# The sign of 64-bit weights placed by one ScalarE rectifier instead of a ScalarE copy and a VectorE max

## The chip, the core and the metric

The kernel runs on one core of one Trainium2 chip. The core has a matrix engine (TensorE, written PE in the profile, with its weight loads as PEld), three engines for elementwise work (VectorE: DVE; ScalarE: ACT; GpSimd: POOL) and a queue that issues the transfers (SyncE: SP). The metric is the time of one execution on the device, in microseconds (us). Lower is better.

## What is computed

Three blocks follow each other over a batch of 4 sequences of 576 tokens: windowed attention with 8 heads of 64, a gated block with a mixing matrix over the sequence, and a squared-rectifier block with a gate. Cut to what matters:

```python
# attention, per batch and head: a band of 128 keys with a linear bias
scores = where(mask, q @ k.T / 8 + bias, -1e9);  attn = softmax(scores);  x = attn @ v
# gated block
h = gelu(x @ w_in); u, v = split(h); v = layernorm(v) * g_ln
x = x + (u * (w_sg @ v + b_sg)) @ w_out
# last block
xk = mu_k * x + (1 - mu_k) * x_prev;  xr = mu_r * x + (1 - mu_r) * x_prev
out = sigmoid(xr @ w_r) * (relu(xk @ w_k) ** 2 @ w_v)
```

The five matrices `w_in`, `w_out`, `w_k`, `w_v` and `w_r` arrive as 64-bit floats. The kernel reads each weight as two 32-bit words, builds a 32-bit float out of them, and splits that into a high and a low part for the matrix engine. Building the 32-bit float is called the decode below.

## The kernel before, in words

The program first records all operations with the tiles that they read and write, then a list scheduler (the planner, `Rec.schedule`) decides at build time in which order each engine runs them and, for operations that may run on several engines, on which. An operation has a cost, a due time worked back from the matrix work that needs it, and a correction from the table `PRI` (lines 29 to 35), which is looked up by the name of the first tile that the operation writes and by its engines. Two entries are of use here: `("st0", "act"): -57000` and `("st1", "act"): 4000` (in ns; a negative one makes an operation more urgent). On the chip each engine runs its list in order and waits where an input or a buffer isn't ready.

Work in the order of time. Attention of batch 0 comes first, alone, with the loads and the decode of `w_in`. Then three rounds follow in which the gated block of batch b runs beside the attention of batch b+1; the decode of `w_out` falls into the first of these. The gated block of the last batch runs with the decode of `w_k`. Last comes the third block in five chunks of tokens (`phase2`), at whose start `w_r` and `w_v` are decoded.

One decode is one call of `job` (line 544) on 128 rows and 512 columns (256 for `w_out`); there are 8 of `w_in`, 8 of `w_out`, 8 of `w_k`, 4 of `w_r` and 8 of `w_v`, 36 in all. `lo` and `hi` are the two words of each weight, interleaved in the loaded tile `raw`. The steps of a job:

- line 548: SP loads `raw`. For `w_in` its place is in the standing tiles `st0` and `st1`; otherwise it is a buffer of a ring (`wraw`).
- line 553: ACT multiplies `hi`, read as a 32-bit float, by 2^-112, in place in `raw`.
- line 554: DVE writes the tile `w` (named `wdec`): the larger of `hf` and `hf * -2^32`, which puts the sign at a bit that survives the next step.
- line 555: DVE shifts `w` left by 3. Line 556: DVE merges the top bits of `lo`.
- line 564: a copy to the high part, on ACT, DVE or POOL; line 565: the rest to the low part, on DVE or POOL.

The tile `wdec` is one of 4 buffers while `w_in` is decoded (a ring that the gated block uses too, tag `t`), one of 2 for `w_out`, and a single buffer for `w_k`, `w_r` and `w_v` (`dec=("raw2", "wdec")`). A job can write it only when the job whose buffer it takes over has finished line 565. In the listing, line 553 doesn't touch `wdec`, so ACT can do it as soon as the load has landed.

Lines of helpers stand for many operations in the rows: L399 is any ACT function of `K.act`, L455 is `stt` (a DVE instruction with two inputs), L472 is `ts` on DVE, L419 is `tt` on DVE, L407 and L409 are copies on ACT and DVE, L427 is a square on ACT, and L377 is every matmul.

Of the kernel before, what the change touches and what calls it, by code (L numbers as in the profile page):

```python
# [13 lines left out]
ACTF = mybir.ActivationFunctionType  # L14
ALU = mybir.AluOpType
# [64 lines left out]
class Vw:  # L80
# [25 lines left out]
    def real(self):  # L106
        t = self.base
        if t.real is None:
            t.real = t.rec.open_pool(t.pool).tile(list(t.shape), t.dtype, tag=t.tag, name=t.name, bufs=t.bufs)
        a = t.real  # L110
        for k, x in self.ops:
            if k == "ix":
                a = a[x]
            elif k == "bc":
                a = a.bitcast(x)
            elif x == 3:
                a = a.rearrange("p a b -> p (a b)")
            elif x == 4:
                a = a.rearrange("p a b c -> p (a b c)")
        return a  # L120
# [374 lines left out]
def attn_gmlp_rwkv_kernel(  # L495
# [18 lines left out]
    nc = tc.nc  # L514
    K = Build(nc)
# [11 lines left out]
    def T(pool, shape, dtype, tag, name=None, bufs=None):  # L527
        return R.tile(pool, shape, dtype, tag, name or tag, bufs)
# [15 lines left out]
    def job(dst_h, dst_l, src, n, dup=False, raw=None, dec=("wraw", "wdec")):  # L544
        if src.dtype != F32:
            if raw is None:
                raw = T(stage[0][0], [P, n, 2], U32, stage[0][1], "wraw")
            K.dma(raw.flat()[:, 0:2 * n], src.bitcast(U32), P * n * 8)
            lo, hi = raw[:, :n, 0], raw[:, :n, 1]
            w = T(dec[0], [P, n], F32, dec[1], "wdec", bufs=4 if dec[0] == "tp" else (2 if dec[0] == "wraw" else 1))  # L550
            wu = w.bitcast(U32)
            hf = hi.bitcast(F32)
            K.act(hf, hf, ACTF.Copy, scale=2.0 ** -112)
            K.stt(w, hf, -(2.0 ** 32), hf, ALU.mult, ALU.max)
            K.ts(wu, wu, 3, None, ALU.logical_shift_left, None)
            K.stt(wu, lo, 29, wu, ALU.logical_shift_right, ALU.bitwise_or, cost=68 + n / 0.96)
        else:
            w = T(stage[0][0], [P, n], F32, stage[0][1], "wraw")
            if dup:
                K.dma(w[0:64], src, 64 * n * 4)  # L560
                K.dma(w[64:128], src, 64 * n * 4)
            else:
                K.dma(w, src, P * n * 4)
        K.copy(dst_h, w, "adp")
        K.sub(dst_l, w, dst_h)
# [8 lines left out]
    def sg_job(kk, half):  # L574
        c = slice(half * HS, half * HS + HS)
        src = w_sgT[kk * P:min(S, kk * P + P), c]
        job(w_sg_t[:, kk, 0, c], w_sg_t[:, kk, 1, c], src, HS, dup=kk == 4)

    def out_job(kk, half):
        c = slice(half * 256, half * 256 + 256)  # L580
        job(w_out_t[:, kk, 0, c], w_out_t[:, kk, 1, c], cols(w_out, kk, half), 256)
# [417 lines left out]
    def phase2(w_k_t):  # L999
# [42 lines left out]
        for kk in range(NC):  # L1042
            job(w_r_t[:, kk, 0, :], w_r_t[:, kk, 1, :], rows(w_r, kk), DM, dec=("raw2", "wdec"))
# [185 lines left out]
```

## Time and profile before

| | us |
|---|---|
| median of 3 runs | 627.09 |
| lowest and highest of them | 625.8, 627.79 |
| the profiled execution, its own time | 628.37 |
| span of the profiled execution | 626.6 |

The span is what the trace covers; 1.77 us of the profiled execution's time lie outside it. Its own time is 1.28 us above the median. Busy times are those of an engine's instructions, without its queue's work. The windows cut the span into stretches by time; the granted clock of TensorE (PEclk) is 1.00 at 2.4 GHz and 0.50 at 1.2 GHz. The chain of waits goes back from the last instruction to whatever released each step.

### The profile page before, as it was taken

How to read it: one execution, taken by the hardware profiler on the slowest of the kernel's cores; microseconds unless marked ns; L12 is line 12 of the kernel's file. 1: busy time of each engine (PE TensorE's matmuls, PEld its weight loads, DVE VectorE, ACT ScalarE, POOL GpSimd, SP SyncE). 2: the span in 40 equal slices, each digit the busy share in tenths (PEclk: the TensorE clock that was granted, in tenths of full speed). 3: DMA queues.
4: the chain of work that ended last, by engine and by line, in shares of the span. 5: the costliest groups of instructions: out<-in, count | busy, mean ns of one | idle time of the engine just before them, and what ended most of it. 6: DMA issues, size and time to landing. Idle time of an engine off the chain costs nothing.

```text
span 626.6 us, 10161 instructions
## 1 busy us (share of the span) xinstructions
PE 595.6 (95%) x3458; PEld 498.7 (80%) x3458; DVE 475.6 (76%) x1286; ACT 352.0 (56%) x912; POOL 189.4 (30%) x348
## 2 busy tenths in 40 slices
PE   8776988997999999999999999899999999999997
PEld 4454867895889998899989998688888887888896
DVE  5888799997999998999689999996384229326122
ACT  5988688785798567883337339744330332234031
POOL 5676375432664354642325430000000001000000
PEclk9987999996999999999999999999999999999999
DMA  8961421432513316010081238433002000000100
GB/s 308 311 218 52 141 69 49 154 94 84 170 56 98 97 40 211 21 61 12 1 274 42 97 112 266 129 109 102 33 2 84 18 0 35 33 1 1 52 18 33
DMA packets 25332, 57.74 MB, mean 92 GB/s; under 512 B 4416, under 2 KB 13120, under 8 KB 24768
## 3 DMA queue, kind: packets, MB, share of 16 engines
q1 hardware_dynamic: 25280, 57.09, 27.7%
q8 instruction: 27, 0.44, 0.3%
q14 instruction: 25, 0.20, 0.1%
HBM read 47.63 MB, written 9.45 MB: 91 GB/s over the span
## 4 chain that ended last, share of the span: by engine, by line
PE 76%; DVE 11%; ACT 7%; DMA 3%; issue 2%; POOL 1%; SPq 0%; POOLq 0%; ACTq 0%; DVEq 0%
PE d L377 41%; PE vps L377 16%; PE rps L377 7%; PE s L377 5%; PE a L377 5%; PE tf L385 2%; ACT p L399 2%; DMA rawqk<-in_qk_dram 2%; DVE p L680 2%; DVE wdec L455 1%; DMA wraw<-in_w_r_dram 1%; ACT pf L407 1%; DVE QK L419 1%; ACT p L482 1%; POOL pf L438 1%
## 5 line engine op out<-in xcount | busy, mean ns | idle before, releaser
L377 PE MATMUL d<-xk,wk 128*128 128x512 f32 (+1 forms) x480 | 105.1, 368 | 0.0
L377 PEld LDWEIGHTS d<-xk,wk 128*128 128x128 f32 x480 | 84.7, 188 | 16.0
L377 PE MATMUL vps<-w_v_t,k2h 128*128 128x512 f32 x288 | 93.9, 396 | 0.0
L399 ACT ACTIVATE p<-p,nmax 128x256 f32<-128x256 f32 (+3 forms) x160 | 76.6, 480 | 24.7 <-DVE nmax L680 23.5
L438 POOL TENSOR_SCALAR_AFFINE_SELECT pf<-pf 128x384 f32<-128x384 f32 (+2 forms) x85 | 51.3, 608 | 50.7 <-ACT pf L407 48.5
L680 DVE CUSTOM_DVE_ANT_0 p<-s,mask 128x256 f32<-128x256 f32 (+3 forms) x160 | 59.9, 380 | 8.4 <-PE s L377 8.2
L377 PE MATMUL d<-w_sg_t,vhl 128*128 128x288 f32 x448 | 65.9, 298 | 0.0
L399 ACT ACTIVATE rl<-d 128x512 f32<-128x512 f32 (+1 forms) x40 | 22.1, 554 | 76.3 <-PE d L377 73.4
L377 PEld LDWEIGHTS vps<-w_v_t,k2h 128*128 128x128 f32 x288 | 54.2, 188 | 12.9 <-DVE r L419 0.3
L377 PE MATMUL d<-w_in_t,xg 128*128 128x512 f32 (+1 forms) x240 | 60.9, 402 | 0.3 <-ACT x L407 0.3
L377 PEld LDWEIGHTS d<-w_sg_t,vhl 128*128 128x128 f32 x448 | 60.7, 188 | 0.6 <-issue 0.2
L377 PE MATMUL d<-gg,w_out_t 128*128 128x288 f32 x384 | 56.8, 299 | 3.6 <-DVE gg L419 3.6
L377 PE MATMUL d<-xg,w_in_t 128*128 128x288 f32 x384 | 56.2, 298 | 1.7 <-DVE u L455 1.3
L377 PE MATMUL rps<-w_r_t,xr 128*128 128x512 f32 x216 | 54.6, 392 | 2.8 <-ACT w_r_t L407 1.4
L377 PE MATMUL vps<-w_v_t,k2l 128*128 128x512 f32 x144 | 57.0, 396 | 0.0
L377 PEld LDWEIGHTS d<-gg,w_out_t 128*128 128x128 f32 x384 | 52.5, 190 | 4.7 <-DVE gg L419 3.9
L409 DVE CAST k2h<-rl 128x512 fp32r<-128x512 f32 (+1 forms) x29 | 11.3, 389 | 59.0 <-ACT rl L427 59.0
L377 PEld LDWEIGHTS d<-xg,w_in_t 128*128 128x128 f32 x384 | 52.1, 188 | 3.2 <-DVE u L455 1.8
L377 PEld LDWEIGHTS d<-w_in_t,xg 128*128 128x128 f32 (+1 forms) x240 | 41.8, 180 | 12.4 <-ACT x L407 0.6
L377 PEld LDWEIGHTS rps<-w_r_t,xr 128*128 128x128 f32 x216 | 40.1, 188 | 12.2 <-ACT w_r_t L407 1.9
L419 DVE TENSOR_TENSOR r<-vps,r 128x512 f32<-128x512 f32 x18 | 12.4, 690 | 46.9 <-PE vps L377 46.8
L421 POOL TENSOR_TENSOR p<-p 128x128 f32<-128x128 f32 (+1 forms) x62 | 33.5, 543 | 38.7 <-ACT p L399 32.3
(119 smaller groups left out, 1176.6 us busy)
## 6 DMA issues: line engine op xcount, KB each, us to landing
rawqk<-in_qk_dram SPq DMA_DIRECT2D x32, 576.0 KB, 4.1
rawv<-in_v_dram SPq DMA_DIRECT2D x32, 160.0 KB, 2.7
xs<-x SPq DMA_DIRECT2D x4, 1154.0 KB, 5.3
out_dram<-r SPq DMA_DIRECT2D x18, 256.0 KB, 2.0
st<-in_w_in_dram SPq DMA_DIRECT2D x8, 512.0 KB, 7.1
wraw<-in_w_k_dram SPq DMA_DIRECT2D x8, 512.0 KB, 3.8
wraw<-in_w_v_dram SPq DMA_DIRECT2D x8, 512.0 KB, 3.5
wraw<-in_w_out_dram SPq DMA_DIRECT2D x8, 256.0 KB, 2.6
```

What stands on the lines that cost most here:

```text
L377: pe.matmul(real(o), real(l), real(r), start=st, stop=sp, **ex)
L385: pe.transpose(real(o), real(i), real(d))
L399: nc.scalar.activation(real(out), real(in_), func, scale=scale, **kw)
L407: alts.append(("act", self._act(in_), lambda: nc.scalar.copy(real(out), real(in_))))
L409: alts.append(("dve", self._dve(in_.n, not in_.ps), lambda: nc.vector.tensor_copy(real(out), real(in_))))
L419: alts.append(("dve", self._dve(out.n, False), lambda: nc.vector.tensor_tensor(real(out), real(a), real(b), op)))
L421: alts.append(("pool", 140 + 2.12 * out.n, lambda: nc.gpsimd.tensor_tensor(real(out), real(a), real(b), op)))
L438: nc.gpsimd.affine_select(out=real(out), in_=real(in_), pattern=[[0, rows], [sgn, n]], compare_op=cmp, fill=0.0, base=0, channel_multiplie ...
L455: alts.append(("dve", cost or self._dve(out.n, False, isinstance(s, Vw)), lambda: nc.vector.scalar_tensor_tensor(real(out), real(a), real( ...
L482: alts.append(("act", self._act(a, 1), lambda: nc.scalar.mul(real(out), real(a), real(s1))))
L680: K.raw("dve", 70 + w / 0.96, lambda: nc.vector.tensor_tensor_reduce(out=real(pw), in0=real(si), in1=real(ma), scale=-0.125, scalar=3.0e38 ...
```

## The change

In `job`, the ACT instruction of line 553 and the DVE instruction of line 554 become one ACT instruction: the leaky rectifier `Prelu`, whose input is `hf` times 2^-112, whose slope for negative inputs is -2^32, and which writes `w`. `raw` isn't written any more after the load. In the record the operation now reads `hf` and writes `wdec`, where line 553 wrote `raw` (`st0`, `st1` or `wraw`). It is given to the planner with the same cost as line 553 had. Nothing else in the text of the kernel changes.

```diff
@@ -550,8 +550,8 @@
             w = T(dec[0], [P, n], F32, dec[1], "wdec", bufs=4 if dec[0] == "tp" else (2 if dec[0] == "wraw" else 1))
             wu = w.bitcast(U32)
             hf = hi.bitcast(F32)
-            K.act(hf, hf, ACTF.Copy, scale=2.0 ** -112)
-            K.stt(w, hf, -(2.0 ** 32), hf, ALU.mult, ALU.max)
+            K.raw("act", K._act(hf), lambda: nc.scalar.activation(
+                real(w), real(hf), ACTF.Prelu, scale=2.0 ** -112, alpha=-(2.0 ** 32)), [hf], [w])
             K.ts(wu, wu, 3, None, ALU.logical_shift_left, None)
             K.stt(wu, lo, 29, wu, ALU.logical_shift_right, ALU.bitwise_or, cost=68 + n / 0.96)
```

## Rows read from the trace of the kernel before

**Rows 1.** The page's busy times: engine, busy us, share of the span, instructions.
```profile
PE 595.6 (95%) x3458; PEld 498.7 (80%) x3458; DVE 475.6 (76%) x1286; ACT 352.0 (56%) x912; POOL 189.4 (30%) x348
```

**Rows 2.** Windows by stage: length, busy PE, PEld, DVE, ACT, POOL, PEclk, DMA.
```profile
0.00:64.00 64.00, 48.61 (x230) 29.70 (x231) 51.28 (x182) 49.72 (x155) 43.37 (x86) 0.87 0.66 219
64.00:100.00 36.00, 32.07 (x198) 25.71 (x198) 32.53 (x90) 28.41 (x77) 20.38 (x41) 0.99 0.28 89
100.00:145.00 45.00, 40.47 (x311) 36.80 (x309) 43.43 (x131) 36.10 (x106) 19.33 (x36) 0.98 0.33 104
145.00:312.00 167.00, 166.58 (x1202) 147.15 (x1204) 150.90 (x450) 115.47 (x340) 77.52 (x150) 0.97 0.25 80
312.00:380.00 68.00, 68.00 (x440) 62.66 (x437) 63.03 (x124) 32.76 (x64) 24.57 (x32) 1.00 0.40 132
380.00:402.00 22.00, 19.15 (x83) 14.92 (x82) 21.34 (x43) 18.90 (x35) 0.00 (x0) 1.00 0.65 208
402.00:627.00 225.00, 220.76 (x1005) 181.80 (x1003) 113.12 (x272) 70.68 (x139) 4.23 (x5) 1.00 0.12 40
```

**Rows 3.** Groups of DVE by shape: count, busy us, mean ns, idle before.
```profile
L455 DVE SCALAR_TENSOR_TENSOR wdec<-wraw 128x512 f32<-128x512 f32 x20 | 13.6, 682 | 0.7 <-ACT wraw L399 0.7
...
L455 DVE SCALAR_TENSOR_TENSOR wdec<-st 128x512 f32<-128x512 f32 x8 | 7.7, 962 | 0.4 <-ACT st L399 0.4
...
L455 DVE SCALAR_TENSOR_TENSOR wdec<-wraw 128x256 f32<-128x256 f32 x8 | 4.9, 609 | 0.0
```

**Rows 4.** Groups of ACT by shape, the same columns.
```profile
L427 ACT ACTIVATE rl<-rl 128x512 f32<-128x512 f32 x32 | 19.9, 632 | 0.8
...
L399 ACT ACTIVATE wraw<-wraw 128x512 f32<-128x512 f32 x20 | 13.6, 682 | 9.2 <-DMA wraw<-in_w_k_dram 6.8 <-DMA wraw<-in_w_v_dram 1.8 <-DMA wraw<-in_w_r_dram 0.7
...
L399 ACT ACTIVATE st<-st 128x512 f32<-128x512 f32 x8 | 5.4, 670 | 0.0
...
L399 ACT ACTIVATE wraw<-wraw 128x256 f32<-128x256 f32 x8 | 3.5, 439 | 0.4 <-DMA wraw<-in_w_out_dram 0.4
...
L399 ACT ACT_TABLE_LOAD x2 | 2.6, 1283 | 0.8 <-PEq L1216 0.8
```

**Rows 5.** Chain of waits, 0 to 64 us, by line.
```profile
by line: ACT p L399 13.1%; PE s L377 13.0%; PE a L377 12.4%; DMA rawqk<-in_qk_dram 7.1%; ACT pf L407 5.6%; issue 5.3%; DVE p L680 5.3%; PE tf L385 5.0%; ACT p L482 4.9%; ACT st L399 4.7%; POOL pf L438 4.0%; DVE p L419 3.2%; ACT x L407 2.0%;
```

**Rows 6.** Chain of waits, 110 to 162 us: by line, then start, us, what.
```profile
by line: PE d L377 12.6%; DVE wdec L455 11.7%; DMA rawqk<-in_qk_dram 9.9%; PE s L377 9.2%; PE a L377 6.1%; DVE w_out_t L419 5.9%; issue 5.7%; DVE p L680 5.5%; ACT QK L407 4.2%; DVE vsg L455 3.9%; PE tf L385 3.3%; DVE gg L419 2.7%; DVE KL L4
...
130.70 1.55 DVE wdec L455
...
136.07 0.67 DVE KL L419
...
136.77 5.17 DMA rawqk<-in_qk_dram
...
142.02 1.15 ACT QK L407
```

**Rows 7.** Timeline of PE: start, us, instruction, idle before it.
```profile
145.06 1.33 PE L377 MATMUL d<-gg,w_out_t 128*128 128x288 f32 x4 [3.62 <-DVE gg L419]
...
396.86 0.73 PE L377 MATMUL rps<-w_r_t,xr 128*128 128x512 f32 x2 [1.44 <-ACT w_r_t L407]
...
400.88 5.74 PE L377 MATMUL rps<-w_r_t,xr 128*128 128x512 f32 x24 [1.23 <-ACT r L399]
```

**Rows 8.** Windows of PE, 2 us each: busy, PEclk, DMA share, GB/s.
```profile
142.00:144.00 2.00, 0.00 (x0) 0.88 0.00 0
144.00:146.00 2.00, 0.94 (x4) 0.50 0.02 4
...
150.00:152.00 2.00, 2.00 (x10) 0.50 0.02 9
...
154.00:156.00 2.00, 2.00 (x21) 1.00 0.38 154
```

**Rows 9.** Timelines of ACT and DVE near 384 us.
```profile
384.39 0.69 ACT L399 ACTIVATE wraw<-wraw 128x512 f32<-128x512 f32 x1
...
384.65 0.68 DVE L419 TENSOR_TENSOR w_r_t<-wdec,w_r_t 128x512 fp32r<-128x512 f32 x1
```

## The prediction, made before the changed kernel was seen

> **What bounds the kernel now.** I read the busy times first [rows 1]. PE is busy for 595.6 of 626.6 us, so all that elementwise work can cost or give back is the remaining 31 us, plus what PE loses at the lower clock. DVE comes second with 475.6 us, but a share of the whole says little here, because the stages have different limits. So I cut the span at the borders of its stages [rows 2]; in each row the reader should subtract PE's busy time from the length, and then see which other engine is full.
>
> - 0 to 64 us: PE idles for 15.4 us. DVE has 51.3 and ACT 49.7 of 64 us; neither is full.
> - 64 to 100: PE idles for 3.9 us, DVE has 32.5 of 36.
> - 100 to 145: PE idles for 4.5 us and DVE is full (43.4 of 45).
> - 145 to 380: PE idles for 0.4 us in 235. Whatever happens on another engine here is hidden, unless it makes PE wait.
> - 380 to 402: PE idles for 2.9 us and DVE is full (21.3 of 22).
> - 402 to the end at 626.6: PE idles for 3.8 us, DVE has half of its time free.
>
> So time is to be had in the first 145 us and around 390 us. Next I read the chain of waits in these stretches. From 0 to 64 us [rows 5] ACT carries more of it than DVE: softmax on ACT (`p` L399 and L482, 18.0% together), copies of `pf` and `x` (7.6%) and the scaling of line 553 (`st` L399, 4.7% of 64 us, or 3.0 us), against 8.5% for the two largest of DVE. From 110 to 162 us [rows 6] it is a DVE chain: the decode's two-input instructions (`wdec` L455) alone are 11.7% of 52 us, which is 6.1 us. At its end stand the low half of the keys (KL) at 136.07 us, a load of `rawqk` that is issued at 136.77, after KL has let go of a buffer, and takes 5.17 us, and the copy to QK at 142.02. Meanwhile PE runs dry: 3.62 us of idle time before 145.06 [rows 7], and behind it the granted clock is 0.50, the lower of its two levels, from 144 to 152 us [rows 8], which costs about half of 8 us, 4.0 us. The two shorter gaps of 1.44 and 1.23 us near 400 us [rows 7] lie in a stage with a granted clock of 1.00 [rows 2].
>
> **What is removed.** The 36 DVE instructions of line 554: 20 of 0.682 us, 8 of 0.962 and 8 of 0.609 [rows 3], 13.6 + 7.7 + 4.9 = 26.2 us of DVE. By stage: the 8 of `w_in` (7.7 us) fall into 0 to 64, the 8 of `w_out` (4.9) into 100 to 145, the 8 of `w_k` (5.5) into 312 to 380, 5 of the third block (3.4) into 380 to 402 and the last 7 (4.8) behind it. The 10.3 us behind 402 and in 312 to 380 are worth nothing in themselves: PE is full there [rows 2]. If that cover went, the 5.5 us of `w_k` would count at most once.
>
> **What is added.** The ACT instructions stay at 36: 20 of 0.682, 8 of 0.670 and 8 of 0.439 us [rows 4]. The function changes and the output is now contiguous, where it had a step of two words. The trace doesn't show the rectifier. Bounds: the square of a contiguous tile of the same size takes 0.632 us and the strided copy 0.682 [rows 4]. I take 0.67, as the input keeps its stride, so ACT's load is the same within 36 x 0.05 = 1.8 us either way, which I leave at 0 in the sum. No load, queue entry of SP or matmul is added or removed.
>
> **What is moved, and the new wait.** The sign step now runs on ACT and writes `wdec`. Line 553 only had to wait for its load: at 384.39 us ACT does it while DVE has yet to finish the job before, at 384.65 [rows 9]. The rectifier must wait until the buffer of `wdec` is free. With 4 buffers (`w_in`) or 2 (`w_out`) that is far off. With the single buffer of the last 20 jobs, each rectifier waits for line 565 of the job before, and behind it in ACT's list stand the rectifiers of the matmul results `d` and, through these, PE. This is the cost that the trace doesn't show. Below: nothing, if the planner gives ACT other work meanwhile. Above: for each of the 4 jobs of `w_r`, one further ACT instruction in front, 0.632 us [rows 4], 2.5 us together on the chain that sets when PE may begin `rps`. Against it, DVE is rid of 3.4 us in the same 22 us, and it is DVE that is full there.
>
> **The plan is made anew.** Durations at build time change, so every list behind the first `w_in` job may come out in another order. Also, the operation is now called `wdec` and misses the two entries of `PRI` for `st0` and `st1`. The four scalings with -57000 were pulled ahead of softmax work; without it they yield to what is due sooner. Since 3.0 us of them lie on the ACT chain [rows 5], I expect no harm from this, but the rows can't exclude it.
>
> **The sum**, against the profiled execution's own time, 628.37 us (the span 626.6 and 1.77 around it):
>
> - 0 to 64 us: the chain is ACT's and PE's for the most part, so of 7.7 us DVE time I count 1.5. Bounds: a gain of 7.7 (all of it was in the way), a loss of 2.4 (the 5.4 us of `w_in` scaling [rows 4] all on the chain instead of 3.0). I take a value near the loss end, as DVE is not full here [rows 2].
> - 100 to 145: DVE is full and the chain is its own, so KL and the load behind it can come up to 4.9 us sooner, more than the gap of 3.62. If the gap closes, so does the stretch at half clock behind it: 3.6 + 4.0 = 7.6 us. I take half, 4.0, since the new order decides whether the buffer of `rawqk` comes free in time. Bounds: 7.6 gain, and a loss of the same 4.0 for one more stretch at half clock elsewhere.
> - 380 to 402: the longer chain of a job and the freed DVE cancel, 0. Bounds: a gain of all 2.9 us of idle time, a loss of 2.5.
> - all else: 0.
>
> Sum: 1.5 + 4.0 + 0 = 5.5 us less, 622.9 us against the execution's own 628.37. That execution was 1.3 us above the median of the runs, so for a median I take 627.09 - 5.5 = 621.6 us. Bounds added up: 7.7 + 7.6 + 2.9 = 18.2 less (608.9) and 2.4 + 4.0 + 2.5 = 8.9 more (636.0).
>
> **The rivals.** *More than that (613 us).* Both early stretches give most of their bound: 6 + 7.6 = 13.6 us. For it: DVE is rid of 7.7 + 4.9 = 12.6 us in these stretches, and the gap before 145.06 us goes back to it [rows 7]. Against it: in the first 64 us ACT is at 78%, and would be next.
>
> *No change (627 us).* The gap at 141 to 145 us stays, because its last link is a transfer of 5.17 us [rows 6], and PE carries on full from 145 on. For it: PE's 95% and the four fifths of the kernel that are PE's alone. Against it: the transfer itself waited for a DVE instruction.
>
> *Slower (632 us): the single buffer.* Place: 371 to 427 us, the 12 jobs of `w_r` and `w_v`. A rectifier that stands in ACT's list before the job ahead has let go of `wdec` stops the evictions of `d` behind it; PE has 4 buffers for these and then stops. Price: 2.5 us until `rps` can start, on top of the 1.44 and 1.23 us which PE waits already, which makes a gap of more than 5 us, as long as the one before 145 us, and so 4.0 us at half clock behind it; together 6.5 us, less 1.5 from the start, +5. It decides as soon as the last low half of `w_r` comes later than now, since PE already waits for it [rows 7]. Against it: 1.00 granted at that place, and DVE's relief. The same mechanism with another place (a gap made by the new order) has the same price.
>
> *The change doesn't work as one instruction (645 us or more).* If the rectifier shared no table with the exponential, each of the 16 jobs of `w_in` and `w_out` would need two table loads of 1.283 us [rows 4], 20.5 us of ACT in either stage. From 0 to 64 us, 49.7 + 20.5 passes 64 by 6; from 100 to 145, 36.1 + 20.5 passes 45 by 12: +18 at least. The trace has two such loads in all, and squares, rectifiers and copies among them need none, so I give it little. The Trainium skill ("ScalarE: Activation LUTs", Table sets: the hidden batching unit) speaks for this danger: it names relu, copy, identity and abs as present in every set, and not the leaky one, and puts a switch with its drain at 2.66 us; by that figure the price would be twice the one above, an estimate. The load's 1.283 us agrees with its figure; no run here shows whether the rectifier needs a load.
>
> **How the numbers follow.** Forecast, a gain of 2 to 11 us (616 to 625): 0.47. More than that: 0.12. No change, within 0.3% (1.9 us, about what a measurement of this kernel tells from no change): 0.16. Slower by the buffer or a new gap: 0.22. Table loads: 0.03. So faster 0.59, same 0.16, slower 0.25. The range takes in the large gain at 611 and the slower rival with its full price, 627.09 + 6.5 = 633.6; it leaves out the table loads and the sums of all bounds, some 1 in 10.
>
> **What would show it right or wrong.** No `wdec` row of L455 with `wraw` or `st` as its only input, 36 rectifiers of about 0.67 us (0.44 for 256 columns), still two table loads, DVE at some 449 us. In 100 to 145 us: no 0.50 clock and no gap of 3 us behind `gg`. If these gaps are there, at another place or the same, the 4.0 us are wrong. In 380 to 402: waits of ACT on DVE's `w_r_t` in place of its waits on loads tell of the slower rival. A first matmul of the gated block that starts later than before means that the lost `PRI` entries mattered. What would make the whole wrong is a new order that moves the gaps for reasons which no row of before shows.

## The result, and the profile of the changed kernel

The changed kernel takes 619.53 us (median of 4 runs, 616.16 to 620.37), against 626.44 us (624.51 to 627.79) for the kernel before: a ratio of 0.9882 with an interval of 0.9835 to 0.9929, 7 us less. The forecast was 621.6 us, so its sign and size came out. Its working holds less well than its sum, as the rest of this document shows.

One caution for every comparison of the two traces: the profiled execution of before (628.37 us) lies 1.9 us above the median of before, and that of the changed kernel (616.16), its fastest, 3.4 us below its own. So the spans differ by 12.2 us (626.6 and 614.4) where the medians differ by 6.9; the other 5.3 us come from which executions were profiled. What makes executions of one program scatter by 4 us stays open.

The busy times of the changed kernel (engine, busy us, share of the span, instructions), beside [rows 1]:

```profile
PE 590.9 (96%) x3458; PEld 495.5 (81%) x3458; DVE 463.0 (75%) x1258; ACT 342.8 (56%) x888; POOL 195.9 (32%) x364
```

PE is idle for 23.5 us of 614.4, where it was 31.0. DVE lost 28 instructions, not 36; ACT lost 24, though the change takes none from it; POOL gained 16. So the planner has moved 24 other operations off ACT. This is a new order with another division of work, not the old one with 36 instructions left out.

The windows by stage (length, busy PE, PEld, DVE, ACT, POOL, PEclk, DMA share, GB/s), cut at the same times as [rows 2]:

```profile
0.00:64.00 64.00, 48.39 (x216) 28.09 (x216) 51.13 (x178) 49.91 (x151) 47.35 (x83) 0.81 0.71 235
64.00:100.00 36.00, 35.23 (x225) 28.51 (x224) 33.80 (x99) 30.25 (x89) 21.91 (x49) 0.96 0.27 83
100.00:145.00 45.00, 42.69 (x340) 39.50 (x341) 43.83 (x132) 33.33 (x98) 23.00 (x45) 1.00 0.33 98
145.00:312.00 167.00, 166.08 (x1210) 147.74 (x1209) 150.37 (x438) 112.85 (x329) 76.13 (x152) 1.00 0.27 86
...
380.00:402.00 22.00, 21.96 (x96) 17.58 (x96) 20.33 (x48) 12.84 (x24) 0.00 (x0) 1.00 0.43 138
```

PE's idle time, length less busy, is 15.6 us (it was 15.4) in the first stage, 0.8 (3.9) in the second, 2.3 (4.5) in the third, 0.9 (0.4) in the fourth and 0.0 (2.9) at 380 to 402 us. DVE is as full as it was from 100 to 145 us (43.8 of 45): the freed time has been filled with other work.

When the parts of the kernel begin tells more than windows do. These are the matmuls of the gated block that read `w_in` and `w_sg`, those of the third block that read `wk`, and the last step of `w_r`'s decode (durations min/median/max in ns, then the first and the last start in us); first the kernel before:

```profile
L377 PE MATMUL d<-w_in_t,xg x240: 388/394/797, 63.2 to 329.5; 128*128 128x512 f32 x96, 128*64 128x512 f32 x24
...
L377 PE MATMUL d<-w_sg_t,vhl x448: 289/295/404, 110.0 to 358.0; 128*128 128x288 f32 x150
...
L377 PE MATMUL d<-xk,wk x480: 274/389/398, 370.1 to 615.5; 128*128 128x512 f32 x128, 128*128 128x256 f32 x32
...
L419 DVE TENSOR_TENSOR w_r_t<-wdec,w_r_t x4: 681/684/691, 384.6 to 397.0; 128x512 fp32r<-128x512 f32 x4
```

and the changed kernel:

```profile
L377 PE MATMUL d<-w_in_t,xg x240: 387/394/502, 67.7 to 320.7; 128*128 128x512 f32 x96, 128*64 128x512 f32 x24
...
L377 PE MATMUL d<-w_sg_t,vhl x448: 289/295/405, 111.2 to 349.2; 128*128 128x288 f32 x150
...
L377 PE MATMUL d<-xk,wk x480: 274/389/428, 361.2 to 603.3; 128*128 128x512 f32 x128, 128*128 128x256 f32 x32
...
L419 DVE TENSOR_TENSOR w_r_t<-wdec,w_r_t x4: 684/685/692, 370.7 to 382.0; 128x512 fp32r<-128x512 f32 x4
```

The gated block begins 4.5 us *later* (67.7 for 63.2), and at 111.2 us the loss is still 1.2. The third block begins 8.9 us earlier. So the gain lies between 110 and 361 us, and as PE is full from 145 us on in both kernels, nearly all of it between 110 us and 152, the end of the half clock in [rows 8]. From its first matmul the third block takes 253.2 us to the span's end (614.4 - 361.2) where it took 256.5: another 3.3 us.

These 3.3 us repeat: the same length is 256.2 to 256.9 us in the traces of before, e1, e4, e5, e7 and e8 below, and 253.0 to 253.8 in those of the changed kernel, e3, e9, e10 and e11 (e2 and e6 stand apart, at 258.8 and 259.6). The 8.9 us hold for this pair of executions only. If the third block is as long in the other executions, the medians leave 6.9 - 3.3 = 3.6 us for everything before it, an estimate.

Windows of PE's work on the tile `d` alone, 110 to 162 us (length, busy and count, PEclk, DMA share, GB/s), before and changed:

```profile
110.00:162.00 52.00, 31.60 (x210) 0.90 0.35 113
```

```profile
110.00:162.00 52.00, 41.10 (x253) 1.00 0.40 131
```

43 more records of gated-block matmuls fit in these 52 us, and the granted clock is 1.00 throughout. The chain of waits of the same stretch in the changed kernel, and SP's loads of `rawqk` there:

```profile
by line: PE d L377 71.6%; PE s L377 10.8%; PE tf L385 5.2%; PE a L377 3.2%; DVE p L680 3.0%; DVE QK L419 2.3%; DVE KL L419 1.3%; DVE x L409 1.2%; issue 1.1%; DVE pf L445 0.4%; DVE nmax L680 0.2%; DVE x L419 0.1%
...
129.45 0.33 SPq L487 DMA_DIRECT2D rawqk<-in_qk_dram  x1
```

In [rows 6] the decode and the load stood on this chain. Now it is PE's own; the load that was issued at 136.77 us goes out at 129.45, behind a KL that DVE does 7.3 us sooner, and the gap and the half clock of [rows 7, 8] are gone.

### The profile page after: what moved, and what is told of

The parts are those of the page before. It is cut to its first block, busy times and chain, and to the rows that moved or that the text cites. A ratio compares the mean times of both kernels' runs of the same rounds, so it can differ in the third digit from the quotient of the medians.

```text
span 614.4 us, 10136 instructions
## 1 busy us (share of the span) xinstructions
PE 590.9 (96%) x3458; PEld 495.5 (81%) x3458; DVE 463.0 (75%) x1258; ACT 342.8 (56%) x888; POOL 195.9 (32%) x364
## 4 chain that ended last, share of the span: by engine, by line
PE 82%; DVE 12%; ACT 3%; issue 1%; POOL 1%; DVEq 0%
PE d L377 46%; PE vps L377 16%; PE rps L377 8%; PE s L377 5%; PE a L377 3%; DVE p L680 2%; PE tf L385 2%; DVE QK L419 2%; DVE KL L419 1%; PE wps L377 1%; DVE vsg L419 1%; ACT p L482 1%; DVE xg L419 1%; DVE vsg L455 1%; DVE p L419 1%
## 5 line engine op out<-in xcount | busy, mean ns | idle before, releaser
L680 DVE CUSTOM_DVE_ANT_0 p<-s,mask 128x256 f32<-128x256 f32 (+3 forms) x160 | 60.0, 381 | 6.1 <-PE s L377 5.4
L421 POOL TENSOR_TENSOR p<-p 128x128 f32<-128x128 f32 (+1 forms) x69 | 39.3, 573 | 42.0 <-ACT p L399 37.4
```

The costliest lines, as they stand in the source:

```text
L421: alts.append(("pool", 140 + 2.12 * out.n, lambda: nc.gpsimd.tensor_tensor(real(out), real(a), real(b), op)))
L680: K.raw("dve", 70 + w / 0.96, lambda: nc.vector.tensor_tensor_reduce(out=real(pw), in0=real(si), in1=real(ma), scale=-0.125, scalar=3.0e38 ...
```

## The experiments

Three theories. A: each DVE instruction that is left out pays where DVE is full, in whatever order the rest runs; so I had reckoned. B: leaving it out is worth nothing in itself, and the planner was led by chance to a better order. C: the time that DVE is rid of pays only through an order that the planner makes for it, so that it takes both.

**e1: the new operation in the old order.** The planner gets the old two operations to plan with; on the chip the first is left out and the rectifier stands in place of the second. The lists of PE, POOL and SP are those of before, line by line; on ACT the rectifier stands where the plan has the maximum, later than the scaling stood. (The lines below show what the edit does; in the kernel both hang on a switch, which is on for all 36 jobs.)

```diff
-            K.act(hf, hf, ACTF.Copy, scale=2.0 ** -112)
-            K.stt(w, hf, -(2.0 ** 32), hf, ALU.mult, ALU.max)
+            K.raw("act", K._act(hf), lambda: None, [hf], [hf])
+            K.raw("dve", K._dve(n, False), lambda: nc.scalar.activation(real(w), real(hf),
+                ACTF.Prelu, scale=2.0 ** -112, alpha=-(2.0 ** 32)), [hf, hf], [w])
```

> The planner is given the two old operations, so that every list of PE, GpSimd and SyncE is that of the kernel before, line by line; only when the instructions are written out is the scaling left away and the rectifier put in the place of the VectorE maximum. Theory A (the relief of VectorE is what pays, in whatever order): about 620 us against 626.4 before; no idle time of PE near 3.6 us before 145 us, and no granted clock of 0.50 at 144 to 152 us. Theory B (the new order is what pays): 626 us within 2, with the gap still there.

625.79 us, a ratio of 0.9996 (0.9975 to 1.0016): nothing. Its page and its PE timeline (start, us, instruction, idle before it), and a window of PE behind it (busy, PEclk):

```profile
PE 594.4 (95%) x3458; PEld 498.1 (80%) x3458; DVE 456.7 (73%) x1250; ACT 352.6 (57%) x912; POOL 186.6 (30%) x348
...
142.79 1.33 PE L377 MATMUL d<-gg,w_out_t 128*128 128x288 f32 x4 [2.56 <-DVE gg L419]
...
393.49 0.73 PE L377 MATMUL rps<-w_r_t,xr 128*128 128x512 f32 x2 [1.42 <-ACT w_r_t L407]
...
144.00:146.00 2.00, 2.00 (x10) 0.50 0.10 25
```

DVE has 36 instructions and 18.9 us less, yet both gaps of [rows 7] stand: 2.56 us for 3.62, and 1.42 for 1.44, with half clock behind the first, if for less long (the granted clock is 0.68 over 144 to 152 us, where it was 0.50). The load of `rawqk` goes out sooner, and what ends the chain of waits before the first gap is now DVE (first SP's loads, then the chain, both start and us):

```profile
134.70 15.20 SPq L487 DMA_DIRECT2D rawqk<-in_qk_dram  x3
...
142.40 0.34 DVE gg L419
```

From 135.65 us to this `gg` the chain holds DVE's instructions alone, in their old order, and no rectifier; before `rps` three rectifiers are on it (at 387.15, 390.86 and 394.38 us), so for that gap e1 doesn't part the old order from the rectifier's later place. As the time doesn't move, theory A falls. The third block of e1 begins at 366.7 us where the trace of before has 370.1, at the same median; so some 3 us of the 8.9 above are scatter between executions.

**e2: the old operations in the new order.** The plan of the changed kernel; each rectifier is written as the copy on ACT, and the maximum on DVE where the plan has the rectifier end.

```diff
-            K.raw("act", K._act(hf), lambda: nc.scalar.activation(
-                real(w), real(hf), ACTF.Prelu, scale=2.0 ** -112, alpha=-(2.0 ** 32)), [hf], [w])
+            o = K.raw("act", K._act(hf), lambda: nc.scalar.activation(
+                real(hf), real(hf), ACTF.Copy, scale=2.0 ** -112), [hf], [w])
+            SECOND[o.i] = lambda: nc.vector.scalar_tensor_tensor(
+                real(w), real(hf), -(2.0 ** 32), real(hf), ALU.mult, ALU.max)
...
```

> The other corner: the plan of the changed kernel, but each rectifier written out as the old scaling on ScalarE at its planned start and the old maximum on VectorE at its planned end. Theory A: VectorE is full again from 80 to 145 us, and 26 us of work come back, so 627 us or more. Theory B: about 620 us as in the changed kernel, since its order is kept.

641.14 us, 1.0241 (1.0212 to 1.0270): much slower than before. Its page, and one of PE's waits (in all, times, the longest):

```profile
PE 598.9 (94%) x3458; PEld 498.9 (78%) x3458; DVE 485.4 (76%) x1294; ACT 343.0 (54%) x888; POOL 199.4 (31%) x364
...
PE s L377 <- DVE nmax L683: 18.1, 16, 4.9
```

DVE now carries the 36 and the 8 that the plan put there. PE's wait for the row maxima of the softmax is 18.1 us, the longest 4.9; in the kernel before it is 10.8 and 2.4. The new order is no better in itself: its plan left no time on DVE for the 36 maxima, and it counts on that time. Theory B in its plain form falls, C stands.

**e3: the two lost entries of the table back.** The changed kernel, with the operation under its old name, so that `st0` and `st1` of `PRI` count again.

```diff
-            K.raw("act", K._act(hf), lambda: nc.scalar.activation(
+            o = K.raw("act", K._act(hf), lambda: nc.scalar.activation(
                 real(w), real(hf), ACTF.Prelu, scale=2.0 ** -112, alpha=-(2.0 ** 32)), [hf], [w])
+            o.lab = raw.base.name
```

> The changed kernel with the rectifiers of w_in planned under the names st0 and st1, so that their two priority entries (-57000 and 4000) count again. If the loss of these entries made the first 64 us slower (first matmul of the gated block at 67.7 us where it was 63.2 before): that matmul at about 63 us and 4 us off the time, some 616 us. If the early loss is due to the clock and the rest of the order: 619.5 us within 2, and the first matmul at 66 us or later.

618.85 us, 0.9884 (0.9860 to 0.9907), as the change. The gated block's first matmul:

```profile
L377 PE MATMUL d<-w_in_t,xg x240: 387/394/502, 68.8 to 322.8; 128*128 128x512 f32 x96, 128*64 128x512 f32 x24
```

It still comes late, at 68.8 us. Putting the entries back changes neither the gain nor the late start; e5 below shows what their loss does to the old operations.

**e4: as e1, in `w_out`'s 8 jobs alone.** Where `new` holds, the two lines of e1 stand, elsewhere the old two.

```diff
+            new = dec[0] == "wraw"
...
```

> The order of the kernel before, as in the first of these, but the rectifier only in the 8 decodes of w_out; the other 28 stay as they were. 4.9 us less of VectorE between 100 and 140 us. If the gap before 145 us hangs on VectorE's chain in that stretch: 622 us or less (the gap of 3.6 us shorter or gone, and the half clock behind it too). If it hangs on the transfer of rawqk or on the order: 626 us.

625.11 us, 0.9982 (0.9968 to 0.9995); the gap before `gg` keeps 2.83 us:

```profile
143.13 1.33 PE L377 MATMUL d<-gg,w_out_t 128*128 128x288 f32 x4 [2.83 <-DVE gg L419]
```

A fixed order gives 0.2% here (0.05 to 0.32%), though these 8 instructions lie just in the stretch that DVE sets.

**e5 and e6: other orders of the old work.** The kernel before, once without the two entries of `PRI` (which stand within a longer line), once with the planner told 40 ns more for each scaling.

```diff
-    ("st0", "act"): -57000, ("st1", "act"): 4000,
```
```diff
-            K.act(hf, hf, ACTF.Copy, scale=2.0 ** -112)
+            K.act(hf, hf, ACTF.Copy, scale=2.0 ** -112, cost=K._act(hf) + 40)
```

> The kernel before with its two operations, but without the priority entries of st0 and st1, which the change loses: a new order of the old work. Theory C (the new order uses the time freed on VectorE; with the old work no order can): 626 us or more, and PE loses as much idle and half-clock time before 160 us as in the kernel before. Theory D (luck of the order: the loss of the two entries alone makes an order without the gap before 145 us): about 619.5 us.

> The kernel before, where the planner is told 40 ns more for each of the 36 scalings of line 553; the instructions are the same. It says how far the time scatters with an order that differs for no reason. Theory C: 626 us within 4, and not 620. Theory D: anything from 618 to 634 us.

628.17 us, 1.0021 (1.0001 to 1.0040), and 629.83 us, 1.0060 (1.0042 to 1.0079). These orders are no near copies of the old one: e5 has 904 instructions on ACT and 354 on POOL, e6 905 and 349, where before has 912 and 348. Their gaps before `gg` shrink, to 1.55 us in e5 and 2.29 in e6, and they gain nothing by it. In e5 the half clock behind that gap is gone as well (two windows with PEclk 1.00, columns as in [rows 2], then the gated block's first matmuls):

```profile
100.00:145.00 45.00, 42.07 (x323) 38.21 (x321) 44.00 (x134) 35.92 (x105) 23.18 (x41) 1.00 0.33 104
145.00:160.00 15.00, 13.48 (x104) 11.50 (x103) 14.65 (x45) 9.63 (x32) 6.74 (x12) 1.00 0.34 108
...
L377 PE MATMUL d<-w_in_t,xg x240: 387/394/568, 68.8 to 327.1; 128*128 128x512 f32 x96, 128*64 128x512 f32 x24
```

So that part of what theory C expected of e5 (as much half clock before 160 us as in the kernel before) missed, though its time came as C had it. What e5 gains there it loses at the start: its gated block begins at 68.8 us, 5.6 us late, with the old operations. e6 loses in the third block, where a new gap of 2.44 us before 426.23 us has half clock behind it (0.59 over 426 to 430 us); that block takes 259.6 us. That other orders of the old work are not better by themselves is what C wants; it is two samples.

**e7, e8, e9 and e10: the change in one group of weights, planned anew.** The condition is `dec[0] == "wraw"` in e7 (`w_out`), `"tp"` in e8 (`w_in`), `"raw2"` in e9 (`w_k`, `w_r`, `w_v`) and `!= "tp"` in e10 (all but `w_in`).

```diff
+            if dec[0] == "wraw":
+                K.raw("act", K._act(hf), lambda: nc.scalar.activation(
+                    real(w), real(hf), ACTF.Prelu, scale=2.0 ** -112, alpha=-(2.0 ** 32)), [hf], [w])
+            else:
+                K.act(hf, hf, ACTF.Copy, scale=2.0 ** -112)
+                K.stt(w, hf, -(2.0 ** 32), hf, ALU.mult, ALU.max)
```

> The rectifier only in the 8 decodes of w_out, planned anew (in the earlier run with the old order this gave 1 us). 4.9 us of VectorE less at 100 to 140 us. Theory C: the gap before 145 us and the half clock behind it go, so about 620 to 622 us. Theory D: no tie between this stage and the result; 624 to 630 us as likely.

e7: 619.86 us, 0.9901 (0.9875 to 0.9926). Where e4 gained 0.2% with the same instructions, a plan made for them gains 1.0%. Its third block begins at 361.3 us, as in the changed kernel, and takes 256.2 us (617.5 - 361.3), as before:

```profile
L377 PE MATMUL d<-xk,wk x480: 274/389/398, 361.3 to 606.4; 128*128 128x512 f32 x128, 128*128 128x256 f32 x32
...
387.73 0.73 PE L377 MATMUL rps<-w_r_t,xr 128*128 128x512 f32 x2 [1.08 <-ACT w_r_t L407]
```

The gap before `rps` is still there, since its decode is the old one.

> The rectifier only in the 8 decodes of w_in, planned anew, with the loss of the two priority entries. 7.7 us of VectorE less before 64 us, none behind it. Theory C: the first 64 us gain little (ACT and the clock bound them) and the gap before 145 us stays: 625 to 628 us. Theory D: anything from 618 to 634 us.

e8: 621.47 us, 0.9910 (0.9878 to 0.9942). Theory C, as I had put it with a stage for each gain, wanted 625 to 628, and missed: `w_in` is decoded in the first 64 us, yet its third block too begins at 361.3 us, if in an execution 2.2 us below its median (619.26 for 621.47), where e7's lies 0.7 below. So the gain before the third block isn't tied to the stage in which the instructions are left out, and it can be had once only.

> The rectifier only in the 20 decodes with the single buffer (w_k, w_r, w_v), planned anew; w_in and w_out decode as before, and PE's list is the one of before until the third block. If these jobs alone remove the idle time of PE near 397 us: gap before 145 us as before, third block (from its first matmul to the end) 253 us in place of 256.5, time 3 us less, 623 us. If the new wait on the single buffer costs what the prediction's slower rival said: 630 us or more.

e9: 623.12 us, 0.9938 (0.9914 to 0.9961). The other way round: the gap of 144 us stays, the third block begins at 369.7 us, nearly as before, and takes 253.0 us (622.7 - 369.7) for 256.5. In the window of 380 to 402 us PE is full:

```profile
144.29 1.33 PE L377 MATMUL d<-gg,w_out_t 128*128 128x288 f32 x4 [3.73 <-DVE gg L419]
...
L377 PE MATMUL d<-xk,wk x480: 274/389/429, 369.7 to 611.6; 128*128 128x512 f32 x128, 128*128 128x256 f32 x32
...
380.00:402.00 22.00, 22.00 (x98) 17.98 (x97) 19.28 (x39) 15.31 (x25) 0.00 (x0) 1.00 0.65 225
```

> The rectifier in the decodes of w_out, w_k, w_r and w_v, planned anew; w_in as before, so the first 60 us are those of the kernel before with its two priority entries in force. If the gains of the two later stages add up: some 8.9 us before the third block, as with w_out alone, and 3 us in it: the changed kernel's time, 618 to 620 us, or less, since its first 64 us were the poorer ones. If either stage's gain was luck of one order: 622 us or more.

e10: 618.42 us, 0.9864 (0.9834 to 0.9894). It has both gains, a third block that begins at 360.6 us (in an execution 3.1 us below the median) and takes 253.0 (613.6 - 360.6):

```profile
L377 PE MATMUL d<-xk,wk x480: 274/389/423, 360.6 to 602.5; 128*128 128x512 f32 x128, 128*128 128x256 f32 x32
```

e7's 0.99% and e9's 0.62% make 1.6%, and e10 has 1.36%, with intervals of 0.3% on each. `w_in` adds nothing to that which shows: the full change has 1.18%.

**e11: another order of the new work.** The changed kernel, with the planner told 40 ns more for each rectifier.

```diff
-            K.raw("act", K._act(hf), lambda: nc.scalar.activation(
+            K.raw("act", K._act(hf) + 40, lambda: nc.scalar.activation(
```

> The changed kernel where the planner is told 40 ns more for each rectifier; the instructions are the same. It says whether the gain holds in another order of the same work. If the freed time on VectorE is what every order can use: 619.5 us within 3. If the changed kernel's order was a lucky one: 624 us or more.

617.89 us, 0.9852 (0.9826 to 0.9879). Four plans for the new work, the change, e3, e11 and e10 (28 of the 36 jobs), lie between 617.9 and 619.5 us; three for the old, before, e5 and e6, between 626 and 630. The gain doesn't hang on one lucky order. None of the variants beats the change by more than the intervals hold.

## Why the prediction came out, point by point

**The whole.** 5.5 us were forecast and 7 measured. By the medians some 3.6 us came before the third block, where 5.5 were forecast, and 3.3 in it, where 0 was. Inside the first sum the start had the wrong sign and the stretch from 64 to 100 us was missing. That these errors made up for each other is luck. The working stood on the old order, and in the old order the change is worth nothing (e1).

**What is removed.** The 36 instructions are gone, but DVE's busy time fell by 12.6 us to 463.0, not by 26.2 to 449. In e1, with just the 36 left out, it fell by 18.9. Some of what stays takes longer there (the shift of 256 columns, 436 ns for 291, is the largest such change): all records of DVE, added up one by one, fall from 556.3 to 532.6 us, by 23.7, which is 2.5 short of the 26.2. The rest of the 7.3 us, 4.8, is overlap: the records of neighbouring instructions overlap, and the busy time counts the overlap once. From e1 to the changed kernel the busy time grows by 6.3 us with the 8 operations that the planner moved to DVE, but they are not all of it: e11 has two instructions more than the changed kernel (1260) and is busy for 457.5 us only. Added up by record the growth is 10.0 us, and 6.1 of them lie in groups with the same count in both, whose instructions take longer.

**What is added.** Of the right size: ACT's groups in the changed kernel (count, busy us, mean ns, idle before and what ended it):

```profile
L553 ACT ACTIVATE wdec<-wraw 128x512 f32<-128x512 f32 x20 | 13.4, 672 | 13.7 <-DVE w_v_t L419 5.9 <-DMA wraw<-in_w_k_dram 3.2 <-DVE wk L419 2.6
...
L553 ACT ACTIVATE wdec<-st 128x512 f32<-128x512 f32 x8 | 5.3, 660 | 0.8 <-DMA st<-in_w_in_dram 0.8
...
L553 ACT ACTIVATE wdec<-wraw 128x256 f32<-128x256 f32 x8 | 3.4, 430 | 0.9 <-DMA wraw<-in_w_out_dram 0.9
...
L399 ACT ACT_TABLE_LOAD x2 | 2.6, 1283 | 0.8 <-PEq L1216 0.8
```

0.67 and 0.44 us were taken, 0.672, 0.660 and 0.430 measured; there are still two table loads, so that rival is out. The Trainium skill ("ScalarE: Activation LUTs", Table sets: the hidden batching unit) doesn't list the leaky rectifier among the functions of every set; here it cost no load.

**0 to 64 us: -1.5 forecast, and a loss came.** The gated block begins 4.5 us later, outside the bounds of -7.7 to +2.4. The step that failed is that I let the old order stand, where only single terms could grow or shrink. The chain of this stretch in the changed kernel (the first of its lines), and PE's windows (busy, PEclk, DMA share, GB/s):

```profile
by line: PE s L377 15.2%; DVE p L680 9.8%; issue 7.1%; PE wps L377 6.7%; PE tf L385 6.5%; POOL w_in_t L421 4.5%; PE a L377 3.9%; ACT p L482 3.7%; DVE p L419 3.5%; DVE QK L419 3.5%; ACT p L399 3.3%; DVE wdec L455 2.9%; DVE sum L472 2.9%; DVE
...
26.00:28.00 2.00, 1.01 (x3) 0.50 0.96 365
...
44.00:46.00 2.00, 1.76 (x6) 0.50 0.05 5
...
60.00:62.00 2.00, 0.94 (x5) 0.50 0.30 74
```

ACT's softmax, 18.0% of the chain in [rows 5], is 7.0%, and the step that makes `p` out of the scores and the mask on DVE (L680) is 9.8% where it was 5.3. So ACT did give way, but the softmax is now held up by DVE and PE, whose idle time is the same, and PE runs at half clock in three stretches (26 to 36, 44 to 52 and 60 to 66 us) instead of two (42 to 48 and 56 to 64). Planning the 8 jobs of `w_in` anew brings the late start: in e10, which leaves these alone, the gated block begins at 61.9 us, in e7 at 62.5, and in e8, which has these only, at 68.0. The rectifier isn't needed for it, nor is the loss of the entries: e5, with the old operations and without the entries, begins at 68.8, and so does e3, with the rectifier and the entries. Which move in the plan does it stays open.

**64 to 100 us: nothing forecast, 3.1 us less idle time.** I had read DVE's 32.5 of 36 us [rows 2] and gone past it. PE's idle time fell from 3.9 to 0.8 us, and this wins back most of what the start lost, as the gated block is 1.2 us late at 111 us.

**100 to 145 us: -4.0 forecast.** The mechanism was right to the row: KL sooner, the load behind it sooner, no gap, no half clock. Its size can't be read off two traces: the third block begins 8.9 us sooner than in the trace of before, and 5.5 sooner than in e1's, which gained nothing, but by the medians 3.6 us. With the 1.2 us by which the gated block is still late at 111 us, this makes some 4.8 us (an estimate), near the 4.0. What makes it was wrong. I took 4.9 us of `w_out` as coming straight off the chain, by half for want of certainty about the order. e1 and e4 take them off and shift the load only from 136.77 to some 134.7 us, as in the old order KL still stands behind the same work, and `gg` behind it keeps its gap. e8 takes off none of them, and its KL stands at 129.52 us, its load at 130.29, and the gap is gone. What counts, I think, is a DVE that falls less far behind by 145 us, and a list that puts KL ahead; that a lead from the first 64 us is carried to 145 fits e8. Both are argued, not shown.

**380 to 402 us: 0 forecast, -3.3 measured** (253.2 us for 256.5), a little past the bound of -2.9. The single buffer does make ACT wait, as the slower rival had it:

```profile
ACT wdec L553 <- DVE w_v_t L419: 5.9, 5, 2.6
...
ACT wdec L553 <- DVE wk L419: 2.6, 6, 1.1
...
ACT wdec L553 <- DVE w_r_t L419: 2.1, 3, 1.1
```

These waits are new, 10.6 us together, with 2.6 the longest. Yet PE is idle for 0.04 us in this stretch. The last step of `w_r`'s decode begins 20.8 us after the first matmul of the third block (382.0 - 361.2) and no longer 26.9 (397.0 - 370.1), so the rival's condition, a last low half that comes later, is not met. In e1, where the order gives no room, it is 27.0 (393.7 - 366.7), and PE waits. I had set DVE's relief against the longer chain one for one; with an order made for it (e9) it is worth more. What the waits still cost would show with a second buffer; no run has one.

**The new order.** Forecast as a risk that could move gaps about; it is the condition of the gain (e1 against e7, e9 and the change). "No harm from the lost entries" is right for the time (e3 with them is no faster than the change, and e5, the old operations without them, 0.2% slower), but not for the start of the gated block in e5. That the kernel can lose time at any place where an order makes a gap is borne out by e6.

**The rivals.** *No change* is what the change does in the old order (e1), and *slower* what the new order does with the old operations (e2), for another reason than the buffer. *More* had the right stretches and for the first of them the wrong sign.

## What to carry to other kernels

Work that is taken from an engine whose list is fixed pays only as far as the order lets what waits behind it move up: here 36 instructions were worth 0.0% in the old order and 1.2% in a new one. So where a planner makes the lists, measure a change both ways, and put its gain down to a stage only when a run with the change in that stage alone has shown it, because backlog can be worked off elsewhere than it arose. Compare parts of two traces only when both executions lie near their medians. To tell a better order from luck, plan the old work and the new several times and see whether the groups of times overlap.

## What the runs showed of the hardware that was not expected

The leaky rectifier with its scale costs ACT no more than the scaled copy did (672 ns for 682 in 20 jobs, 430 for 439 in 8), and it runs among exponentials and other functions with the same two table loads of 1283 ns. And the same busy time of PE can hold less work: in the first 64 us the changed kernel has 22 us of windows with a granted clock of 0.50 to 0.55, the kernel before 14, at 48.4 and 48.6 us of busy time with 216 and 230 matmul records.
